# Weight scales found in groups, and low parts of weights on GpSimd, in a four-layer attention kernel

## The chip, the cores and the metric

The kernel runs on one core of one Trainium2 chip. TensorE (PE in the profile; PEld are its weight loads), VectorE (DVE), ScalarE (ACT), GpSimd (POOL) and SyncE (SP, which here only issues DMAs) each take their own queue of instructions in order. The metric is the device time of one execution, in microseconds.

## The reference, cut to what matters

```python
x = A_x                                     # (1, 2048, 512)
x = x + _A_ref(_layernorm(x), A_wqkv, A_wo) # 32 heads of 16, 8 keys at distance 0, 2, .. 14
x = x + _B_ref(_layernorm(x), B_wqkv, B_wo) # 32 heads of 16, the last 256 keys
x = x + _A_ref(_layernorm(x), A_wqkv, A_wo)
x = x + _B_ref(_layernorm(x), B_wqkv, B_wo)
return x
```

Each of the two attentions projects the normalised x with `wqkv` (512 x 1536), takes a softmax over its window and projects back with `wo` (512 x 512). All is in float32.

## The kernel before, in words

The 2048 positions are cut into eight chunks of 256. A float32 matrix product is made of three float16 ones: each factor is split into a high part and a low part (the rest), and high x high, high x low and low x high are summed. To split a weight, it is first scaled by a power of two near its largest value.

**The work is a list of tasks.** `plan.add(engine, us, function, r=, w=)` adds a task with the values that it reads and writes. Every task has a place number in the table `ORDER`, by scope and in the order in which the tasks were added; an engine takes its tasks by rising place. A negative number, -1 - place, also gives the task to its second engine (`alt=`). `plan.order()` then puts the five queues into one program and hands out buffers and PSUM banks. So `ORDER` fixes what every engine does and when. The scopes are `pA` and `pB` (the preparation of the two pairs of weights, function `prep`, line 766), `W` (110 idle tasks), and `A0`, `B0`, `A1`, ... `B15`: An and Bn are the steps of `layer_a` (line 1019) and `layer_b` (line 1184) for chunk n mod 8 of the first (n < 8) or second pair of layers.

**The idle tasks** (`idle`, line 1496) are three matmuls each on the constant `selt`, into a bank that nobody reads. `selt` is built by GpSimd at the start (lines 747 to 752), after the other constants.

**Preparation.** `prep(T)` handles four weight matrices, s = 0, 1, 2 (the three parts of `wqkv`: Q, K, V) and 3 (`wo`), each in two halves j of 128 x 1024 elements:

- `load` (line 785) brings a half to SBUF. For s < 3 it is staged in the stacks `stk[j, s]`, which B's attention uses later. For s = 3 it goes to a buffer of the pool `pp6`, which has three. A and B use the same staging, so a load for B waits until the task that last read A's half is done.
- `squares` (line 805, ScalarE or VectorE) sums the squares of each partition into one column of `am`. Its unused full output goes to the place of the low part.
- Two PE transpositions (line 818) bring the two columns of 128 sums into one row of 256 on one partition.
- `one` (lines 821 to 830), six small VectorE instructions, takes the maximum, makes a power of two of its root, and from it two factors. A PE matmul with `ones` (line 833) spreads them to 128 partitions, and `factors` (line 837) copies them into `psc`.
- For s = 1 and 3, `both_scales` (line 844) makes the product of two scales that a later step needs.
- `split` makes the high part (line 861 on ScalarE, 863 on VectorE) and then the low part (line 865, always VectorE): low = weight x factor - high, one instruction of 1024 elements (two of 512 for B's s = 0 and 1).

**Around it.** `norm` (line 876) takes statistics (L889, L892, L895), a power on GpSimd (`rstd`, L898), a shift (L901), normalises (`xnorm`, L916, into the pool `pxn` with one buffer), transposes on PE (L920) and splits (L925, L926). `proj_t` (L945 to L947) and `proj_n` (L965 to L968) are the projections; each waits for all high and low parts of its matrix. In `layer_a` the products of q and k (L1078) come in four groups of four, each summed on PE (L1086); then maximum, difference, exponential, sum, reciprocal and scaling (L1109 to L1121; in chunk 0 behind a copy, L1099, and a select, L1102), a split of the result (L1142, and the rest, `erest`, L1129), eight weighings of v (`weigh`, L1168) from PSUM banks that PE spreads, each summed over the window by `total` on VectorE (L1173) or GpSimd (L1175 to L1177), and the output projection in `finish` (L988 to L996). In `layer_b`, K and Q go through DRAM into the stacks by SyncE's DMAs (L1209, L1220); zero rows are written to the stacks once (`put`, L1487), after A's and B's staged weights have left them.

Of the kernel before, what the change touches and what calls it, by code (L numbers as in the profile page):

```python
# [10 lines left out]
BF16 = mybir.dt.bfloat16  # L11
# [4 lines left out]
ALU = mybir.AluOpType  # L16
# [24 lines left out]
    "pA": [2, -7, 1, 0, 4, 3, 7, 7, 9, 7, 13, 6, 12, 3, 2, 4, 3, 6, 8, 10, 11, 14, 22, 10, 17, 11, 18, 6, 8, 5, -9,  # L41
        15, 10, 16, 25, 20, 17, 34, 14, 27, 7, 12, 10, 15, 43, 41, 39, 59, 44, 46, 27, 53, 24, 76],
    "pB": [15, 19, 9, 18, 61, 60, 52, 72, 54, 39, 80, 29, 61, 13, 26, 14, 25, 77, 75, 60, 92, 62, 63, 35, 92, 41, 85,
        17, 23, 16, 22, 89, 69, 65, 109, 71, 43, 93, 37, 94, 18, 36, 12, 31, 102, 93, 72, 113, 74, 78, 42, 98, 40,
        84, 20, 31, 23, 3, 19, 21, 20, 22],
    "W": [12, 71, 79, 83, 101, 136, 2, 84, 100, 87, 86, 73, 137, 88, 111, 16, 0, 1, 144, 141, 90, 13, 142, 125, 105,
        124, 96, 106, 95, 104, 126, 139, 112, 98, 107, 68, 123, 91, 110, 135, 145, 14, 76, 103, 138, 119, 266, 310,
        218, 251, 239, 273, 244, 265, 260, 274, 272, 263, 275, 278, 285, 268, 269, 238, 319, 253, 256, 315, 448, 436,
        3432, 3433, 3412, 3489, 3438, 3466, 3471, 3431, 3464, 3469, 3491, 3499, 3490, 3488, 3505, 3484, 3480, 3582,
        3580, 3576, 3589, 3587, 3586, 3585, 3570, 3584, 3575, 3577, 3571, 3581, 3583, 3572, 3560, 3579, 3496, 3511,  # L50
        3512, 3502, 3588, 3578],
    "A0": [0, 0, 2, 1, 3, 4, 2, 5, 1, 5, 5, 11, 4, 9, 9, 15, 0, 1, 17, 18, 19, 20, 21, 22, 23, 24, 34, 38, 40, 42,
        46, 47, 48, 51, 13, 20, 26, 27, 28, 29, 30, 31, 32, 33, 35, 36, 37, 39, 45, 49, 50, 52, 16, 21, 54, 55, 56,
        57, 58, 63, 66, 82, 64, 65, 67, 74, 78, 80, 81, 85, 32, 33, 5, 7, 31, 30, 33, 32, 44, 38, 36, 37, 35, 53, 43,
        40, 41, 42, 62, 50, 51, 49, 48, 70, 28, 6, 55, 56, 30, 57, 58, 59, 34, -9, 94, 64, 9, 66, 10, 97, 68, 11, 67,
        -70, 108, 70, 12, 73, 14, 99, 77, 15, 75, -80, 38, 13, 114, 115, 116, 117, 118, 120, 121, 122, 81, 44, -83,
        127, 128, 129, 130, 131, 132, 133, 134, 86],
    "B0": [83, 88, 87, 89, 90, 18, 91, 46, 143, 48, 97, 45, 140, 47, 95, 147, 150, 153, 154, 155, 157, 161, 165, 151,
        156, 158, 159, 163, 164, 166, 169, 53, 103, 54, 102, 24, 25, 29, 28, 26, 27, 33, 43, 38, 40, 148, 168, 170,
        175, 180, 184, 185, 186, 149, 162, 167, 171, 174, 176, 178, 179, 56, 105, 55, 104, 30, 35, 32, 37, 34, 36,  # L60
        39, 42, 41, 44, 241, 243, 247, 249, 250, 252, 255, 258, 65, 240, 248, 257, 259, 262, 267, 270, 276, 67, 246,
        133, 226, 124, 245, 132, 222, 118, 221, 119, 237, 128, 225, 125, 242, 135, 138, -140, 140, 45, 46, 279, 68,
        288, 70, 32, 309, 280, 69, 286, 72, 33, 311, 74, 282, 152, 295, 157, 283, 149, 277, 146, 287, 154, 292, 155,
        281, 151, 284, 150, 158, 73, 160, 47, 48, 322, 82, 323, 80, 35, 397, 372, 90, 380, 91, 37, 413, 99, 318, 174,
        324, 178, 300, 161, 313, 170, 316, 172, 321, 176, 312, 171, 314, 173, 179, -181, 181, 49, 50, 411, 98, 395,
        94, 40, 458, 404, 96, 407, 97, 39, 463, 111, 299, 168, 345, 186, 379, 194, 374, 193, 353, 189, 373, 192, 344,
        185, 354, 188, 195, -197, 197, 67, 69, 432, 103, 426, 100, 41, 443, 440, 106, 439, 107, 43, 453, 109, 76, 72,
        77, 78, 258, 79, 80, 271, 270, 123, 56, 503, 504, 505, 506, 507, 508, 509, 510, 286, 83, 125, -284, 512, 515,
        516, 518, 519, 520, 521, 522, 293, 84],
    "A1": [8, 21, 24, 19, 23, 26, 4, 28, 49, 146, 50, 100, 51, 152, 52, 101, 16, 17, 160, 173, 177, 182, 187, 189,  # L70
        190, 191, 196, 197, 202, 203, 205, 207, 208, 213, 57, 60, 172, 181, 183, 188, 192, 193, 194, 195, 198, 199,
        200, 201, 204, 209, 211, 212, 58, 59, 210, 214, 216, 217, 219, 223, 228, 232, 220, 227, 229, 230, 231, 233,
        235, 236, 61, 62, 21, 23, 108, 106, 109, 107, 206, 111, 113, 110, 112, 215, 114, 115, 117, 116, 224, 122,
        120, 121, 123, 234, 126, 127, 63, 129, 130, 131, 64, 134, 254, 137, 26, 136, 25, 261, 141, 27, 142, -144,
        264, 144, 28, 145, 30, 271, 148, 31, 147, -154, 66, 29, 289, 290, 291, 293, 294, 296, 297, 298, 159, 71,
        -157, 301, 302, 303, 304, 305, 306, 307, 308, 163],
    "B1": [162, 164, 165, 166, 167, 34, 169, 75, 317, 77, 175, 76, 320, 79, 177, 328, 329, 337, 339, 341, 342, 343,
        347, 326, 327, 330, 332, 333, 334, 335, 338, 86, 187, 85, 184, 56, 55, 54, 53, 52, 51, 64, 68, 61, 71, 336,
        349, 350, 352, 356, 358, 360, 361, 340, 346, 348, 351, 355, 357, 359, 365, 87, 190, 88, 191, 57, 60, 59, 58,
        62, 63, 65, 66, 70, 73, 418, 430, 435, 438, 441, 442, 445, 446, 108, 451, 452, 455, 457, 460, 461, 462, 464,  # L80
        112, 444, 232, 233, 415, 219, 221, 416, 218, 220, 412, 212, 213, 403, 206, 207, 427, 223, 225, 433, 226, 229,
        449, 235, 237, 239, 110, 241, 74, 75, 478, 118, 476, 117, 52, 488, 470, 115, 485, 120, 53, 499, 473, 116,
        469, 114, 55, 500, 498, 124, 486, 122, 57, 525, 132, 450, 236, 240, 472, 256, 260, 459, 244, 246, 454, 242,
        247, 477, 261, 263, 467, 249, 251, 468, 252, 254, 471, 255, 259, 264, 121, 272, 81, 82, 530, 133, 524, 130,
        59, 549, 526, 131, 532, 134, 60, 550, 562, 143, 541, 137, 62, 607, 542, 139, 561, 144, 63, 608, 153, 501,
        280, 284, 523, 294, 295, 531, 296, 297, 513, 289, 291, 502, 281, 285, 487, 267, 269, 497, 275, 277, 514, 288,
        290, 298, 135, 299, 86, 87, 600, 151, 581, 148, 64, 619, 620, 158, 610, 154, 66, 636, 616, 156, 638, 162, 71,
        652, 635, 160, 627, 159, 70, 653, 169, 553, 310, 312, 554, 311, 313, 568, 315, 318, 609, 333, 335, 601, 326,
        327, 605, 328, 329, 548, 305, 308, 569, 319, 321, 336, 157, 339, 104, 105, 644, 164, 646, 165, 73, 671, 654,
        168, 657, 170, 77, 682, 658, 171, 670, 174, 78, 683, 675, 176, 669, 175, 80, 687, 179, 106, 109, 114, 115,  # L90
        387, 116, 117, -90, 403, 188, 90, 724, 725, 726, 727, 728, 729, 730, 731, 417, 120, 190, -416, 733, 734, 735,
        737, 738, 739, 742, 743, 420, 121],
    "A2": [11, 45, 47, 25, 29, 96, 19, 99, 78, 325, 83, 182, 81, 331, 84, 183, 22, 24, 362, 363, 364, 366, 367, 368,
        369, 370, 376, 385, 387, 389, 390, 392, 393, 394, 89, 93, 371, 375, 377, 378, 381, 382, 383, 384, 386, 388,
        391, 398, 399, 400, 401, 402, 92, 95, 408, 409, 410, 417, 419, 420, 424, 428, 406, 421, 422, 423, 429, 431,
        434, 437, 101, 104, 36, 42, 199, 201, 198, 200, 396, 203, 204, 202, 205, 405, 211, 209, 208, 210, 414, 215,
        216, 214, 217, 425, 222, 224, 102, 227, 228, 230, 105, 231, 447, 234, 44, 238, 45, 456, 245, 47, 243, 46,
        465, 250, 51, 248, 48, 466, 253, 50, 257, -263, 113, 49, 474, 475, 479, 480, 481, 482, 483, 484, 265, 119,
        -267, 489, 490, 491, 492, 493, 494, 495, 496, 273],
    "B2": [268, 274, 276, 278, 279, 58, 282, 126, 511, 127, 287, 128, 517, 129, 292, 527, 528, 529, 533, 534, 535,  # L100
        536, 537, 538, 539, 540, 543, 544, 545, 546, 547, 136, 300, 138, 307, 88, 89, 92, 93, 90, 91, 99, 94, 107,
        110, 552, 558, 567, 570, 571, 572, 573, 574, 551, 555, 556, 559, 560, 563, 564, 565, 147, 320, 145, 316, 95,
        101, 98, 97, 100, 96, 103, 102, 108, 111, 642, 647, 655, 659, 660, 661, 662, 665, 172, 667, 668, 672, 673,
        674, 676, 677, 679, 177, 664, 364, 366, 634, 348, 349, 639, 351, 353, 626, 344, 345, 621, 342, 343, 651, 358,
# [1433 lines left out]
```

## Time and profile before

| | us |
|---|---|
| median of the runs shown (1453.41 to 1456.76, 3 runs) | 1454.05 |
| the profiled execution's own time | 1453.95 |
| its span, from the first to the last instruction | 1451.9 |
| busy: PE / DVE / ACT / POOL | 1355.8 / 1207.2 / 735.7 / 662.3 |
| mean granted TensorE clock | 0.974 |

In rows of the timeline the first number is the start in us from the span's start and the second the busy time; `x4` is a run of four instructions; a bracket gives the idle time ahead on that engine and what ended it. In rows of groups the last parts are the busy us, the mean ns of one, and the idle time ahead. In rows of the chain that ended last, the numbers are start and length.

### The profile page before, as it was taken

The numbers are of one execution on the slowest core, as the hardware profiler recorded it, in microseconds if no ns is written. First come the engines' busy times: TensorE is split into PE (matmuls) and PEld (weight loads), VectorE is DVE, ScalarE is ACT, GpSimd is POOL, SyncE is SP. The second block draws the span as 40 slices with busy tenths as digits, with TensorE's granted clock in tenths as the row PEclk, the third lists the DMA queues.
The fourth block names the chain that finished last, engine by engine and source line by source line (L and its number), as shares of the span: only waits on it lengthen the run. The fifth ranks groups of instructions, "written<-read, shape, count | busy, mean of one in ns | idle before, by whom it ended". The sixth has DMA issues, their size and how long they took to land.

```text
span 1451.9 us, 35262 instructions
## 1 busy us (share of the span) xinstructions
PE 1355.8 (93%) x14058; PEld 792.8 (55%) x14058; DVE 1207.2 (83%) x2311; ACT 735.7 (51%) x1049; POOL 662.3 (46%) x756
## 2 busy tenths in 40 slices
PE   7798999999899998989989998999999999999998
PEld 5474645647365563746547364654647456474554
DVE  7959698797979979697887969898797988979794
ACT  6522345554554555555554444454454555545564
POOL 2505054372734618363471716356272542737333
PEclk9998999999999999999999999999999999999999
DMA  7031122212221221222122231212212132132221
GB/s 261 16 79 32 54 49 73 65 51 82 55 75 49 63 83 36 92 45 77 45 63 81 55 100 32 85 51 68 75 48 94 24 82 69 44 90 55 72 67 46
DMA packets 89221, 97.40 MB, mean 67 GB/s; under 512 B 34016, under 2 KB 60128, under 8 KB 89056
## 3 DMA queue, kind: packets, MB, share of 16 engines
q1 hardware_dynamic: 88800, 94.89, 23.5%
q8 instruction: 110, 1.80, 0.5%
q14 instruction: 55, 0.45, 0.1%
q10 hardware_dynamic: 256, 0.26, 0.1%
HBM read 50.33 MB, written 35.09 MB: 59 GB/s over the span
## 4 chain that ended last, share of the span: by engine, by line
PE 57%; DVE 24%; POOL 6%; issue 5%; ACT 3%; DMA 3%; SPq 1%; DVEq 0%; POOLq 0%; ACTq 0%
PE banks L945 10%; PE banks L947 9%; PE banks L946 9%; PE banks L1389 6%; DVE m L1281 5%; PE banks L1086 4%; DVE banks L1285 4%; DVE pw L1168 4%; PE banks L1357 3%; PE banks L967 3%; PE banks L1263 3%; PE banks L965 3%; PE banks L968 2%; PE banks L920 2%; POOL pw L1175 2%
## 5 line engine op out<-in xcount | busy, mean ns | idle before, releaser
L1363 ACT ACTIVATE p<-banks,sclB 128x768 f32<-128x768 f32 x480 | 420.6, 900 | 250.1 <-PE banks L1359 203.5
L1372 POOL TENSOR_SCALAR_AFFINE_SELECT p<-p 128x1024 f32<-128x1024 f32 x240 | 262.9, 1102 | 411.2 <-ACT p L1363 387.2
L1281 DVE TENSOR_REDUCE m<-banks 128x2 f32<-128x512 f32 x448 | 299.7, 688 | 5.2
L1285 DVE COPY_PREDICATED banks<-maskt,banks 128x256 f32<-128x256 int16 x448 | 181.4, 424 | 67.3 <-PE banks L1266 53.8
L1078 DVE TENSOR_TENSOR pr<-kv,q 128x512 f32<-128x512 f32 x232 | 164.2, 761 | 44.0 <-ACT kv L1059 16.3
L1389 PE MATMUL banks<-p,v 128*32 128x128 f32 (+1 forms) x3840 | 196.8, 331 | 3.4 <-POOL p L1372 2.5
L1357 PE MATMUL banks<-stk,stk 64*128 64x256 f16 x960 | 136.2, 281 | 27.4 <-DVE m L1281 10.3
L1389 PEld LDWEIGHTS banks<-p,v 128*32 128x32 f32 x3840 | 106.7, 109 | 98.5 <-issue 38.8
L1168 DVE TENSOR_TENSOR pw<-banks,kv 128x1024 f32<-128x1024 f32 x128 | 153.1, 1215 | 2.6 <-PE banks L1155 1.4
L1175 POOL TENSOR_TENSOR pw<-pw 128x512 f32<-128x512 f32 x101 | 129.4, 1281 | 19.8 <-DVE pw L1168 19.3
L1266 PE MATMUL banks<-stk,stk 48*128 48x128 f16 (+1 forms) x1024 | 125.6, 248 | 3.6 <-DVE m L1277 0.9
L1263 PE MATMUL banks<-stk,stk 48*128 48x128 f16 (+1 forms) x896 | 111.0, 252 | 17.4 <-DVE m L1281 7.5
L1357 PEld LDWEIGHTS <-stk 64*128 64x128 f16 x960 | 56.0, 94 | 113.6 <-issue 109.4
L1359 PE MATMUL banks<-stk,stk 64*128 64x128 f16 x960 | 108.4, 220 | 0.0
L1263 PEld LDWEIGHTS <-stk 48*128 48x128 f16 x896 | 49.7, 94 | 95.5 <-issue 91.8
L916 ACT ACTIVATE xn<-x,rs 128x512 f32<-128x512 f32 x64 | 52.1, 814 | 66.4 <-DVE rs L901 55.7
L1176 POOL TENSOR_TENSOR pw<-pw 128x256 f32<-128x256 f32 x101 | 73.9, 731 | 7.9
L1086 PE MATMUL banks<-pr,sel 128*32 128x512 f32 x512 | 70.2, 603 | 1.8 <-DVE pr L1078 1.7
L945 PE MATMUL banks<-xh,wA0h 128*128 128x256 f16 x256 | 70.3, 275 | 1.3 <-DVE xl L926 1.3
L945 PE MATMUL banks<-xh,wB1h 128*128 128x256 f16 x256 | 70.7, 276 | 0.0
L945 PE MATMUL banks<-xh,wA2h 128*128 128x256 f16 x256 | 70.5, 275 | 0.1
L947 PE MATMUL banks<-xh,wB1l 128*128 128x256 f16 x256 | 70.4, 275 | 0.0
(184 smaller groups left out, 3066.2 us busy)
## 6 DMA issues: line engine op xcount, KB each, us to landing
stk<-re SPq DMA_DIRECT2D x256, 96.0 KB
re<-eh SPq DMA_DIRECT2D x128, 128.0 KB
re<-el SPq DMA_DIRECT2D x64, 128.0 KB
oc<-os SPq DMA_DIRECT2D x120, 64.0 KB
os<-scr SPq DMA_DIRECT2D x15, 512.0 KB
x<-in_A_x_dram SPq DMA_DIRECT2D x8, 512.0 KB
xd<-x SPq DMA_DIRECT2D x16, 256.0 KB
x<-xd SPq DMA_DIRECT2D x8, 512.0 KB
```

Source lines behind the costliest of these rows:

```text
L945: nc.tensor.matmul(ps[mp].t[:, i], wh, xh, start=k == 0, stop=False)
L947: nc.tensor.matmul(ps[mp].t[:, i], wl, xh, start=False, stop=k == 3)
L1078: E.tensor_mul(pr.t, window(kv[1].t, m, 64 * tq, 64)[:, 0], qb)
L1168: nc.vector.tensor_mul(pw.t, pb.t.unsqueeze(1).broadcast_to([P, 2, W, 64]), v)
L1175: E.tensor_add(t[:, :, 0:4], t[:, :, 0:4], t[:, :, 4:8])
L1263: nc.tensor.matmul(ps.t[:, par, 0 : (2 - qb) * P], lhs, stk[hf, bef][r, col, qb * P :], start=True, stop=True)
L1281: nc.vector.tensor_reduce(out=m.t[:, :, u, qb], in_=ps.t[:, :, 0 : 2 * P], op=ALU.max, axis=AX.X)
L1285: nc.vector.copy_predicated(t[:, :, 0:P], maskt[:, 0:P].bitcast(I16).unsqueeze(1).broadcast_to([P, 2, P]), t[:, :, 2 * P : 3 * P])
L1357: nc.tensor.matmul(o[:, two], k[:, jf * P : (jf + 1) * P], q, start=True, stop=True)
L1363: nc.scalar.activation(pt.t[:, :, 2 * i : 2 * i + 2].rearrange("p s m q -> p m s q"), ps.t[:, :, : 3 * P].rearrange("p m (s q) -> p m s q" ...
L1372: nc.gpsimd.affine_select(out=v, in_=v, pattern=[[0, 8], [-1 if b == 0 else 1, P]], compare_op=ALU.is_gt if b == 0 else ALU.is_ge, fill=0. ...
L1389: nc.tensor.matmul(o, v[:, jj, 17 * h : 17 * h + 32], rhs, start=z == 0 and (b == 0 or first), stop=z == 1 and b == 1, tile_position=(0, 3 ...
```

## The change

1. **Scales in groups.** `SCALES` names the groups: for A {0}, {1} and {2, 3}, for B all four. A group of n has one `am` of 128 x n x 2. A new VectorE task `most` takes the larger of the two columns of each matrix, one transposition brings n columns to n partitions, and `one` works on n partitions at once. For n > 1 it ends with a product with the identity, which puts the n pairs of factors on a diagonal, and one matmul with n rows of ones spreads all of them. One `factors` copies them. So there are four rounds in place of eight, and no matrix of a group has its scale before all the squares of the group are there.
2. **Low parts.** The low part has GpSimd as a second engine, in two instructions: the weight is scaled in place, then the high part subtracted. `ORDER` picks it for four of the sixteen: A's s = 0, j = 1, and B's s = 2 (both halves) and s = 3, j = 1.
3. **Orders.** All tables of `ORDER` are new. Outside `pA` and `pB`, 30 tasks go from GpSimd to VectorE, 26 from VectorE to GpSimd, 12 from ScalarE to VectorE and 9 the other way. In `A0` two products and one sum go to GpSimd, and two sums and `erest` to VectorE.

```diff
 ORDER = {
-    "pA": [2, -7, 1, 0, 4, 3, 7, 7, 9, 7, 13, 6, 12, 3, 2, 4, 3, 6, 8, 10, 11, 14, 22, 10, 17, 11, 18, 6, 8, 5, -9,
-        15, 10, 16, 25, 20, 17, 34, 14, 27, 7, 12, 10, 15, 43, 41, 39, 59, 44, 46, 27, 53, 24, 76],
...
-    "W": [12, 71, 79, 83, 101, 136, 2, 84, 100, 87, 86, 73, 137, 88, 111, 16, 0, 1, 144, 141, 90, 13, 142, 125, 105,
-        124, 96, 106, 95, 104, 126, 139, 112, 98, 107, 68, 123, 91, 110, 135, 145, 14, 76, 103, 138, 119, 266, 310,
...
+    "pA": [1, 0, 2, -7, 7, 19, 8, 23, 9, 8, 16, 5, -3, 3, 2, 4, 3, 10, 27, 12, 33, 15, 19, 10, 18, 9, 17, 7, 11, 5, -12,
+        8, 12, 10, 13, 29, 58, 35, 73, 40, 25, 47, 24, 48, 41, 26, 51, 23, 46],
+    "pB": [11, 16, 13, 17, 12, 18, 14, 20, 17, 29, 18, 30, 15, 19, 16, 27, 54, 93, 59, 105, 62, 37, 74, 42, 85, 64, 40,
+        86, 36, 78, 44, -19, 38, -24, 65, 35, 87, 39, -21, 24, 29, 30, 1, 22, 20, 19, 21],
+    "W": [32, 10, 34, 24, 12, 77, 1, 82, 8, 3, 6, 13, 30, 17, 9, 35, 38, 14, 31, 129, 5, 25, 128, 75, 4, 76, 22, 28, 36,
+        21, 107, 79, 0, 26, 18, 15, 125, 2, 83, 78, 126, 37, 80, 7, 16, 11, 234, 252, 207, 258, 268, 259, 303, 240,
...
 }
+SCALES = {"A": ((0,), (1,), (2, 3)), "B": ((0, 1, 2, 3),)}
...
-    ones = cst.tile([1, P], F32, name="ones")
+    ones = cst.tile([4, P], F32, name="ones")
...
+            am = buf("psm", [P, 4, 2], F32, "am", f"am{T}{some[0]}")
...
+            def most(am=am, ax=ax, n=n):
+                nc.vector.tensor_reduce(out=ax.t[:, 0:n], in_=am.t[:, 0:n], op=ALU.max, axis=AX.X)
+
+            plan.add("DVE", 0.12, most, r=vam, w=[vax])
+            plan.add("PE", 0.3, lambda pt=pt, ax=ax, n=n: nc.tensor.transpose(pt.t[0:n, 0:P], ax.t[:, 0:n], idf), r=[vax], w=[vpt])
+
+            def one(pt=pt, a1=a1, n=n):
+
+                b = a1.t[0:n]
+                a = b[:, n]
+                nc.vector.tensor_reduce(out=a[:, 0:1], in_=pt.t[0:n, 0:P], op=ALU.max, axis=AX.X)
...
+                if n > 1:
+                    nc.vector.tensor_tensor(out=b[:, 0:n], in0=b[:, n : n + 1].broadcast_to([n, n, 2]),
+                                            in1=idf[0:n, 0:n].unsqueeze(2).broadcast_to([n, n, 2]), op=ALU.mult)
+
+            def spreads(pt=pt, a1=a1, n=n):
+                v = a1.t[0:n, 0:n] if n > 1 else a1.t[0:1, 1:2]
+                nc.tensor.matmul(pt.t[:, 2 * P : 2 * P + 2 * n], ones[0:n], v.rearrange("p a b -> p (a b)"), start=True, stop=True)
...
+                        for t, h, lo in parts:
+                            if low and which is nc.gpsimd:
+                                which.tensor_scalar(t, t, sc, None, op0=ALU.mult)
+                                which.tensor_tensor(out=lo, in0=t, in1=h, op=ALU.subtract)
+                            elif low:
+                                which.scalar_tensor_tensor(lo, t, sc, h, op0=ALU.mult, op1=ALU.subtract)
...
-                plan.add("DVE", 1.15, lambda f=split: f(None), r=[*touched[j], vsc[s], vh, vlow[j]], w=[vwt[T, s]])
+                    plan.add("DVE", 1.19, lambda E, f=split: f(E, True), r=[*touched[j], vsc, vh, vlow[j]], w=[vwt[T, s]], alt=("POOL", 3.7))
```

In the new tables pA's tasks are, in order: for each group its loads and squares, `most`, the transposition, `one`, the matmul, `factors`, and then for each matrix `both_scales` (s = 1 and 3) and the two pairs of high and low part. So the sixth number of `pA`, 19, is the place of the first transposition on TensorE, and its last, 46, that of the low part of s = 3, j = 1 on VectorE.

157 lines of the change are left out of this document (80 added, 77 removed), and 819 rows, old and new, of the table ORDER.

## The prediction

> **What bounds the kernel now.** I read the page first, then the busy times of long stretches, then the chain that ended last.
>
> ```profile
> PE 1355.8 (93%) x14058; PEld 792.8 (55%) x14058; DVE 1207.2 (83%) x2311; ACT 735.7 (51%) x1049; POOL 662.3 (46%) x756
> ...
> 0.00:90.00 90.00, 69.11 (x462) 45.28 (x463) 72.65 (x148) 48.98 (x72) 31.94 (x59) 0.94 0.38 118
> ...
> 720.00:810.00 90.00, 85.40 (x908) 49.60 (x906) 74.17 (x153) 47.87 (x68) 44.93 (x51) 0.96 0.26 69
> ```
>
> The columns of the stretches are busy us of PE, PEld, DVE, ACT, POOL, then the granted clock and the DMA share. From 90 us on TensorE is busy 85 of 90 us. Only the first 90 us, where the weights are prepared, leave it idle for 21 us. Nothing but orders changes after that, so the sum is made in those 90 us, at the marks of the chain that ended last and of the timeline:
>
> ```profile
> 52.72 1.28 POOL pw L1175
> ...
> 55.34 1.24 POOL pw L1175
> ...
> 70.18 0.80 POOL o L1177
> 71.00 0.63 ACT oh L988
> ...
> 77.37 0.71 POOL rs L898
> ...
> 84.04 0.11 PE banks L945
> ```
> ```profile
> 17.39 0.42 PE L945 MATMUL banks<-xh,wA0h 128*128 128x256 f16 x1
> ...
> 26.67 2.47 DVE L1078 TENSOR_TENSOR pr<-kv,q 128x512 f32<-128x512 f32 x4
> ...
> 34.05 2.50 DVE L1078 TENSOR_TENSOR pr<-kv,q 128x512 f32<-128x512 f32 x4 [0.23 <-PE banks L1086]
> ...
> 39.50 0.69 DVE L1078 TENSOR_TENSOR pr<-kv,q 128x512 f32<-128x512 f32 x1
> ...
> 41.36 0.58 ACT L1099 COPY e<-banks 128x512 f32<-128x512 f32 x1 [0.43 <-PE banks L1086]
> ...
> 43.02 1.08 DVE L1109 TENSOR_REDUCE mx<-e 128x64 f32<-128x512 f32 x1 [0.49 <-POOL e L1102]
> ...
> 51.43 1.21 DVE L1168 TENSOR_TENSOR pw<-banks,kv 128x1024 f32<-128x1024 f32 x1
> ```
>
> These are A0's Q projection, its first and third groups of products, its maximum, its first weighing, its sums on GpSimd (to 70.98), and B0's norm and projection. From 84 us TensorE is full, so what moves 84.04 moves the end.
>
> **What is taken away.** Durations:
>
> ```profile
> 40.10 0.40 DVE L824 TENSOR_REDUCE a1B<-banks 1x1 f32<-1x256 f32 x1
> ...
> 41.21 1.25 DVE L865 SCALAR_TENSOR_TENSOR wA3l<-stageA,pscA,wA3h 128x1024 f16<-128x1024 f32 x1
> ```
> ```profile
> L1175 POOL TENSOR_TENSOR pw<-pw 128x512 f32<-128x512 f32 x101 | 129.4, 1281 | 19.8 <-DVE pw L1168 19.3
> L1372 POOL TENSOR_SCALAR_AFFINE_SELECT p<-p 128x1024 f32<-128x1024 f32 x240 | 262.9, 1102 | 411.2 <-ACT p L1363 387.2
> ```
> ```profile
> L990 POOL TENSOR_TENSOR ol<-o,oh 128x512 f16<-128x512 f32 x1 | 1.2, 1157 | 0.0
> ```
> ```profile
> L1173 DVE TENSOR_REDUCE o<-pw 128x128 f32<-128x1024 f32 x2 | 3.8, 1918 | 0.0
> ...
> L990 DVE TENSOR_TENSOR ol<-o,oh 128x512 f16<-128x512 f32 x1 | 0.7, 693 | 0.3 <-ACT oh L988 0.3
> ...
> L837 DVE COPY pscA<-banks 128x2 f32<-128x2 f32 x4 | 0.6, 145 | 0.0
> ```
>
> One `one` holds VectorE from 40.10 to 41.21, 1.11 us. Eight become four: two of about 1.0 (half the columns) and two of about 1.15 (one product more), and four `most` of about 0.15 each are added (the copy of L837 is the nearest row): 8.9 us become 4.9. Four copies in `factors` go, 0.5. Four low parts of 1.25 go to GpSimd, 5.0. Against it, A0 takes one sum more on VectorE (1.9) and one rest (0.7) and gives two products away (1.2). VectorE so loses some 8 us of the first 90. TensorE loses twelve transpositions and four small matmuls, behind other work. On GpSimd a low part is two instructions over 1024 elements that the trace does not show. The subtraction is two of the 512-element form, 2.6 us; the scaling lies between the 1.1 of the select over 1024 elements and 2.6. So it costs 3.7 to 5.2 us, and up to 9.1 if every element goes as slowly as in the 2.27 us row below. I take 4.1, near the quiet rows.
>
> **What is moved.** The new `ORDER["W"]` holds every place from 0 to 18, and pA's first transposition has place 19: 19 idle tasks, 57 matmuls, stand ahead of it on TensorE, which takes its queue in order. Before, three tasks do.
>
> ```profile
> 7.45 2.10 PE L1498 MATMUL banks<-selt 128*128 128x256 f16 x9 [7.45 <-POOL selt L751]
> ...
> 9.35 0.89 PE L818 MATMUL banks<-idf,amA 128*1 128x128 f32 x2
> ```
> ```profile
> 57.32 1.16 PE L1498 MATMUL banks<-selt 128*128 128x256 f16 x9
> ...
> 64.23 0.61 PE L965 MATMUL banks<-wA3h,ol 128*128 128x512 f16 x1 [1.14 <-POOL ol L990]
> 64.63 0.63 PE L967 MATMUL banks<-wA3h,oh 128*128 128x512 f16 x1
> 65.06 0.63 PE L968 MATMUL banks<-wA3l,oh 128*128 128x512 f16 x1
> ...
> 69.11 1.85 PE L1498 MATMUL banks<-selt 128*128 128x256 f16 x12
> ```
>
> The idle matmuls read `selt`, which GpSimd finishes at 7.4, and nothing that the diff touches comes earlier. At half clock they start every 0.225 us (9 in 2.10, the last lasting 0.27), at full clock every 0.111. From 64.23 TensorE worked some 4.9 us before it was granted full speed. So the head of the queue is 4.9 us with 22 matmuls and 35 at 0.111, 3.9 us, and ends at 16.2; all at full clock it would end at 13.8, all at half at 20.3. The Trainium skill (TensorE: Matmul & The Clock Gate, Part 1) has the array run at half rate until about 3.4 us of sustained activity in a free-running window; by it the head would end between 15.4 and 17.1. This trace's 4.9 us agrees with the upper part.
>
> Behind the head wait the first transposition, `one` on VectorE with all that follows it there, and A0's second `xnorm` on ScalarE, since `pxn` has one buffer that the first transposes must free.
>
> **The steps,** each against its mark (ScalarE's squares, splits and copies by these rows, loads by the DMA row):
>
> ```profile
> L808 ACT ACTIVATE wA1l<-stk 128x1024 bf16<-128x1024 f32 x2 | 2.1, 1040 | 0.0
> L861 ACT ACTIVATE wA1h<-stk,pscA 128x1024 f16<-128x1024 f32 x2 | 2.2, 1140 | 0.4 <-DVE pscA L837 0.4
> L1059 ACT ACTIVATE kv<-banks 128x512 f32<-128x512 f32 x4 | 2.2, 585 | 0.0
> ```
> ```profile
> 24.00:26.00 2.00, 2.00 (x20) 1.78 (x19) 1.90 (x3) 2.00 (x4) 1.20 (x1) 1.00 1.04 310
> ```
> ```profile
> 0.81 0.46 SPq L1028 DMA_DIRECT2D x<-in_A_x_dram  x1
> ...
> 4.72 1.29 DVE L889 BATCH_NORM_STATS2 b<-x 128x6 f32<-128x512 f32 x2 [4.72 <-DMA x<-in_A_x_dram]
> ```
>
> 1. Q projection. Transposition to 16.6, `one` to 17.6, matmul behind two idle tasks and A0's transposes, factors at 18.2. ScalarE: split 18.3 to 19.5, copy, copy (second transposes done at 20.4), second split 21.1 to 22.2, VectorE's low part to 23.5. GpSimd's low part runs from 19.6 to 23.7. Start 23.8, **+6.4**.
> 2. First products. K's first half is complete after 17 tasks of three matmuls at 0.11, at 29.4, the copy at 30.0, product at 30.1; VectorE, after three low parts and four statistics, arrives there too. +3.4, so **-3.0**: two low parts and one `one` are gone, and chunk 2's x is loaded sixth, so that nothing waits for it.
> 3. Third group. ScalarE must square five halves of B's weights before it copies the second half of q and k. Their loads wait for low parts that free the staging: the first for 23.5, the next four for 25.9. At 310 GB/s a load of 512 KB takes 1.7 us; the first x, issued by 1.3, was there at 4.7, so landing adds 1.8. The fifth is there at 34.6. Two squares of 1.04 and two copies follow: 38.1, +4.0, so **+0.6**.
> 4. Maximum. Third group 2.5, three low parts 3.75 and two products 1.25 bring VectorE to 45.6; the last product to the copy of e took 1.2 us (40.2 to 41.36). But the copy stands behind B's eighth square, whose load needs the buffer that the first of these low parts frees at 41.8: there at 46.2, squared at 47.3. Copy and select to the maximum took 1.66: 49.0, +6.0, so **+2.0**.
> 5. First weighing. 8.4 us before. The 2.2 us low part and the wait behind it go; the rest on VectorE and its wait for the copy come to 1.3: 7.4 us, 56.4, so **-1.0**. B's `most` stands in this stretch ahead of the sum of e and all that follows; its last squares end near 50.2, while VectorE is still at `less` to 50.7, which hides it.
> 6. Last sum. Before 19.55 us, with six sums and one rest on GpSimd. Five sums of 2.6 and the rest, starting 1.25 after the weighing, with 0.6 for a buffer and 0.5 for contention: 16.4 us, 72.8 against 70.98, so **-3.2**.
> 7. B0's projection. The 6.4 us from 70.98 to 77.37 stay: GpSimd's low part ahead of `rstd` starts after a copy and a split (1.8 us) and ends at 5.9. Only one idle task is left between the last reduction and B0's transposes, where 34 were, so A0's first output half runs cold, 12 matmuls at 0.43 (64.63 to 65.06), 5.1 us, and pushes the second by 0.8. Low parts on both engines add 0.5 (below). **+1.3**.
>
> Sum: 6.4 - 3.0 + 0.6 + 2.0 - 1.0 - 3.2 + 1.3 = +3.1 at 84 us.
>
> ```profile
> 63.51 1.75 DVE L865 SCALAR_TENSOR_TENSOR wA3l<-stageA,pscA,wA3h 128x1024 f16<-128x1024 f32 x1
> ...
> 64.13 2.27 POOL L1175 TENSOR_TENSOR pw<-pw 128x512 f32<-128x512 f32 x1
> ...
> 92.39 2.54 SPq L1209 DMA_DIRECT2D re<-eh  x4
> ```
>
> A low part beside GpSimd work took 1.75 us for 1.25, and GpSimd 2.27 for 1.28. The Trainium skill (GPSIMD Engine Reference, 1. Specifications) says that GpSimd shares its SBUF interfaces with VectorE and contends with instructions of two SBUF inputs, which speaks against moving low parts there while others stay. These two rows agree; the contention in steps 6 and 7 is priced by them.
>
> SyncE: the zero rows of B0's stacks are queued ahead of K's writes and wait for GpSimd's last low part. `rstd` ends at 80.2; a low part of 4.1, a copy and A2's `rstd` of 0.95, and another 4.1 make 89.4, eight writes of about 0.65 follow, partly done by then, to about 93. K's writes, at 92.39 before, are ready at 95.5. Hidden by 2 us, and lost above 5.2 us for a low part.
>
> **The rest.** Outside the preparation 30 tasks go from GpSimd to VectorE and 26 back, 21 small ones move between ScalarE and VectorE, and neighbours swap places. No row prices this. Of 90 us some 5 are idle on TensorE in the steady part; a tenth of that, won or lost, in each of 15 stretches is 7 us at the most. I take 0.
>
> The profiled execution took 1453.95 us (span 1451.9 and 2.05 around it), 0.1 below the median of 1454.05. Forecast: 1453.95 + 3.1 = **1457.0**.
>
> **The rivals.**
> A. The head is shorter or hidden. For each us that the first transposition comes before 16.2 the start gains one; at 13.8 it is 1454.6, and without the loads' +0.6 and half of the +2.0 1453.0. For it: the loads, not TensorE, hold ScalarE. Against it: 7.45 is a releaser that the trace names.
> B. Faster: the new order of the later stretches wins what the start loses. TensorE's idle time is cut by 0.5 us of the 5 in each of 15 stretches, 7.5 us: 1449.5. It beats the start from 0.2 us per stretch on. Or the head costs nothing at all: the first transposition is then at 10.1, every mark 6.1 us earlier and the time 1451, 1448 if steps 3 and 4 come to nothing with it.
> C. Slower by more: the staging buffer. `pp6` has three; A's two halves of wo and B's first take them. If B's second half waits for the half whose low part comes last (after the last products, 47.1), its load lands at 51, its square ends at 52.2, and the copy of e, queued behind it on ScalarE, comes 4.9 us later: 1462. It decides only if the low part of the other half (place 46 of `pA`) does not free the buffer.
>
> **How the numbers follow.** About 0.2% (2.9 us) is what a measurement of this kernel can tell from no change. Forecast (1454.6 to 1460) 0.50, of which 0.20 lies below 1456.96; A (1451.1 to 1454.6) 0.14; B (below 1451.1) 0.19; C (above 1460) 0.17. So faster 0.19, same 0.34, slower 0.47. The range reaches to B's and C's middle and a little beyond: 1448 to 1463.
>
> **What would show it.** The head: the first transposition (L818 before) near 16, with 57 idle matmuls from 7.45, and the Q projection near 23.8; if it starts before 18, step 1 is wrong. ScalarE waiting for B's loads near 30 to 34 shows step 3. The first weighing at 56, the last sum at 73 and B0's projection at 87 show the rest. If these hold and the end does not, B is right; a copy of e near 53 shows C. A low part above 5.2 us on GpSimd, with K's writes waiting for zero rows, would make the forecast too low.

## The result, and the profile after

| | before | after |
|---|---|---|
| median (runs, range), us | 1454.63 (4, 1453.41 to 1456.76) | 1470.03 (4, 1468.98 to 1472.79) |
| profiled execution / its span, us | 1453.95 / 1451.9 | 1472.79 / 1471.1 |
| granted TensorE clock, mean of the profiled execution | 0.974 | 0.955 |

The ratio is 1.0107 (95% interval 1.0094 to 1.0120): the changed kernel is 15.6 us slower. The forecast was 1457.0, the range ended at 1463. The profiled execution of after is the slowest of its four, 18.8 us above that of before.

The same long stretches as in the prediction, in the changed kernel:

```profile
0.00:90.00 90.00, 58.75 (x382) 37.37 (x382) 67.24 (x116) 47.15 (x69) 43.93 (x61) 0.85 0.36 114
720.00:810.00 90.00, 85.37 (x918) 50.64 (x918) 75.30 (x140) 45.89 (x66) 44.16 (x50) 0.96 0.23 62
```

VectorE did get lighter in the first 90 us, by 5.4 us where some 8 were forecast (72.65 to 67.24), and GpSimd heavier (31.94 to 43.93). But TensorE did 10 us less in that time (69.11 to 58.75), and its granted clock fell from 0.94 to 0.85. The steady stretch is as full as before (85.40, 85.37).

TensorE's timeline of after. The 57 idle matmuls of the head run from 7.47; the first transposition follows at 16.38; the Q projection starts at 23.01, stops 1.13 us for GpSimd's low part and 0.47 us for one of VectorE's; B0's projection starts at 91.48, at 0.21 us per matmul, twice the 0.11 of full speed. That is what "half clock" means below:

```profile
7.47 9.07 PE L1523 MATMUL banks<-selt 128*128 128x256 f16 x57 [7.47 <-POOL selt L749]
16.38 0.27 PE L831 MATMUL banks<-idf,axA 128*1 128x128 f32 x1
...
23.01 0.27 PE L970 MATMUL banks<-xh,wA0h 128*128 128x256 f16 x1
...
25.17 0.28 PE L972 MATMUL banks<-xh,wA0l 128*128 128x256 f16 x1 [1.13 <-POOL wA0l L884]
...
27.45 0.28 PE L972 MATMUL banks<-xh,wA1l 128*128 128x256 f16 x1 [0.47 <-DVE wA1l L886]
...
91.48 0.40 PE L970 MATMUL banks<-xh,wB0h 128*128 128x256 f16 x1 [2.54 <-DVE xl L951]
...
92.24 0.42 PE L972 MATMUL banks<-xh,wB0l 128*128 128x256 f16 x1
92.45 0.42 PE L970 MATMUL banks<-xh,wB1h 128*128 128x256 f16 x1
```

VectorE's timeline, at the marks of the prediction. Low parts (L886) that take 1.27 us alone (48.60) take 2.2 on average at 23.04 and at 43.15:

```profile
23.04 4.35 DVE L886 SCALAR_TENSOR_TENSOR wA1l<-stk,pscA,wA1h 128x1024 f16<-128x1024 f32 x2
...
31.35 1.29 DVE L1103 TENSOR_TENSOR pr<-kv,q 128x512 f32<-128x512 f32 x2 [0.18 <-ACT kv L1084]
...
39.50 2.53 DVE L1103 TENSOR_TENSOR pr<-kv,q 128x512 f32<-128x512 f32 x4 [1.72 <-ACT kv L1084]
...
43.15 4.32 DVE L886 SCALAR_TENSOR_TENSOR wA2l<-stk,pscA,wA2h 128x1024 f16<-128x1024 f32 x2
...
48.60 1.27 DVE L886 SCALAR_TENSOR_TENSOR wA3l<-stageA,pscA,wA3h 128x1024 f16<-128x1024 f32 x1
...
52.07 1.04 DVE L1134 TENSOR_REDUCE mx<-e 128x64 f32<-128x512 f32 x1 [2.20 <-POOL e L1127]
...
59.51 1.23 DVE L1193 TENSOR_TENSOR pw<-banks,kv 128x1024 f32<-128x1024 f32 x1
...
79.52 1.45 DVE L886 SCALAR_TENSOR_TENSOR wB1l<-stk,pscB,wB1h 128x512 f16<-128x512 f32 x2
...
84.06 2.26 DVE L886 SCALAR_TENSOR_TENSOR wB0l<-stk,pscB,wB0h 128x512 f16<-128x512 f32 x2
86.20 3.38 DVE L886 SCALAR_TENSOR_TENSOR wB1l<-stk,pscB,wB1h 128x512 f16<-128x512 f32 x2
...
90.74 1.28 DVE L951 TENSOR_TENSOR xl<-banks,xh 128x512 f16<-128x512 f32 x2
```

GpSimd's timeline: a low part is 2.85 us of scaling (L883) and 2.12 to 2.52 of subtraction (L884), 5.0 to 5.4 together; two of A0's products (42.70) take 3.69 us together; the last sum ends at 76.26; B0's `rstd` waits behind a low part:

```profile
19.66 2.86 POOL L883 TENSOR_SCALAR stk<-stk,pscA 128x1024 f32<-128x1024 f32 x1 [10.84 <-ACT wA0h L888]
22.60 2.52 POOL L884 TENSOR_TENSOR wA0l<-stk,wA0h 128x1024 f16<-128x1024 f32 x1
...
42.70 3.69 POOL L1103 TENSOR_TENSOR pr<-kv,q 128x512 f32<-128x512 f32 x2 [2.42 <-PE banks L1111]
...
75.81 0.45 POOL L1202 TENSOR_TENSOR o<-pw 128x128 f32<-128x128 f32 x1
78.06 2.85 POOL L883 TENSOR_SCALAR stk<-stk,pscB 128x1024 f32<-128x1024 f32 x1 [1.80 <-ACT wB2h L888]
81.00 2.12 POOL L884 TENSOR_TENSOR wB2l<-stk,wB2h 128x1024 f16<-128x1024 f32 x1
83.22 0.72 POOL L923 TENSOR_TENSOR rs<-rs,mhalf 128x2 f32<-128x2 f32 x1
...
94.55 2.13 POOL L884 TENSOR_TENSOR wB2l<-stk,wB2h 128x1024 f16<-128x1024 f32 x1
```

After 92 us the distance still grows. One exponential of A (L1138 before, at 44.9 to 1311.6 us) marks each of the 16 chunks; in after the sixteen are:

```profile
L1163 ACT ACTIVATE e<-e,sclA x16: 711/722/722, 53.9 to 1324.6; 128x512 f32<-128x512 f32 x16
```

Each number is how much later the exponential of that chunk starts than before, in order: 9.0, 10.9, 12.3, 10.9, 13.2, 13.4, 13.7, 14.7, 13.1, 13.2, 12.7, 14.1, 12.5, 12.5, 11.1 and 13.0 us. The spans end 19.2 apart. So the loss of this execution comes in three parts: 9 us up to A0's maximum, 4 us from there to the steady chunks, and 6 us in the last 150 us. In that last part the closing projection waits 3.11 us for ScalarE and starts at half clock (0.43 us per matmul, then 0.21). Before, it waited 1.09 us and ran at 0.22 from its first matmul. Rows of after, and one of before:

```profile
1460.27 0.61 PE L992 MATMUL banks<-wB3h,oh 128*128 128x512 f16 x1 [3.11 <-ACT oh L1013]
...
1462.80 0.63 PE L992 MATMUL banks<-wB3h,oh 128*128 128x512 f16 x1
...
1464.09 0.38 PE L993 MATMUL banks<-wB3l,oh 128*128 128x512 f16 x1
```
```profile
1442.41 0.39 PE L967 MATMUL banks<-wB3h,oh 128*128 128x512 f16 x1 [1.09 <-ACT oh L988]
```

### The profile page after: what moved, and what is told of

The parts are those of the page before. It is cut to its first block, busy times and chain, and to the rows that moved or that the text cites. A ratio compares the mean times of both kernels' runs of the same rounds, so it can differ in the third digit from the quotient of the medians.

```text
span 1471.1 us, 35151 instructions
## 1 busy us (share of the span) xinstructions
PE 1361.9 (93%) x14038; PEld 797.9 (54%) x14038; DVE 1199.4 (82%) x2292; ACT 734.8 (50%) x1046; POOL 675.9 (46%) x758
## 4 chain that ended last, share of the span: by engine, by line
PE 31%; DVE 12%; DMA 3%; issue 3%; ACT 2%; POOL 1%; SPq 1%; ACTq 0%; POOLq 0%; DVEq 0%
PE banks L970 5%; PE banks L971 4%; PE banks L972 4%; PE banks L1414 4%; DVE m L1306 3%; PE banks L1382 2%; DVE banks L1310 2%; PE banks L992 2%; DVE pw L1193 2%; PE banks L993 2%; PE banks L1111 2%; PE banks L990 2%; PE banks L1288 2%; ACT p L1388 1%; PE banks L945 1%
## 5 line engine op out<-in xcount | busy, mean ns | idle before, releaser
L972 PE MATMUL banks<-xh,wA2l 128*128 128x256 f16 x256 | 70.5, 275 | 2.2 <-DVE wA2l L886 2.2
L970 PE MATMUL banks<-xh,wB0h 128*128 128x256 f16 x256 | 70.1, 274 | 2.5 <-DVE xl L951 2.5
L1224 DVE SCALAR_TENSOR_TENSOR el<-banks,eh 128x512 f16<-128x512 f32 x64 | 43.4, 686 | 33.9 <-ACT eh L1221 33.4
```

Source lines behind the costliest of these rows:

```text
L970: nc.tensor.matmul(ps[mp].t[:, i], wh, xh, start=k == 0, stop=False)
L972: nc.tensor.matmul(ps[mp].t[:, i], wl, xh, start=False, stop=k == 3)
```

## The experiments

All ran beside the kernel before, whose median was 1453.35 to 1455.34 on the chips used, so ratios are compared; an excess in us is the ratio's part over 1, times 1455. A bracket behind a ratio is its 95% interval; 0.001 of it is 1.5 us. Kernels named b_ start from the kernel before, best_try and the others from the changed one, except late_only (its text says how it is made). Line numbers in their rows differ by a few. Diffs of `ORDER` are given as queues.

**Where in time.** The orders are cut where both kernels have done the same 322 tasks.

```diff
 late_only:  preparation, first 322 tasks: before;  rest of ORDER:
-            before
+            after
 early_only: preparation, first 322 tasks: after;   rest of ORDER:
-            after
+            before
```

> The kernel before, with its own preparation and its own order for the first 322 tasks outside preparation (up to B0's scores, some 105 us), and the changed kernel's orders for all that follows. Theory: most of the loss is made before that point (the offset of the marks is +10.8 us at B0's exponential and +13 at the steady chunks), so the later orders alone cost 3 to 5 us: 1458 to 1460 us. Rival 1, the later orders are neutral, as predicted: 1454 to 1456. Rival 2, the later orders lose it all and a late start would have been made up: above 1464.

> The changed kernel's preparation, low parts on GpSimd and order up to the same point, then the orders of the kernel before. Theory: the start keeps its +11 us: 1464 to 1467. Rival 1 (later orders neutral): 1468 to 1471, as the changed kernel. Rival 2 (a late start is made up): 1454 to 1458.

late_only: 1459.2 us, ratio 1.0024 (1.0012 to 1.0036), +3.5 us. early_only: 1468.6, 1.0091 (1.0078 to 1.0104), +13.2. Most of the loss is made in the preparation and the orders up to the cut, as the theory had it, and it is not made up. The later orders cost the kernel before 3.5 us (1.7 to 5.2), where the prediction took 0. Taking them back from the changed kernel wins 2.4, which the intervals do not tell from nothing: early_only missed its theory (1464 to 1467) and lies in the range of the rival that calls the later orders neutral.

**The head.**

```diff
 no_head, TensorE's queue:
-idle x19, transposition of A's s = 0
+idle x3,  transposition of A's s = 0       (IDLE = 94)
 b_head:
-idle x3,  transpositions of A's s = 0
+idle x19, transpositions of A's s = 0      (IDLE = 126)
 after_selt:
     nc.gpsimd.memset(mhalf, -0.5)
+    selt = ... (its six lines, moved up from behind sel4)
```

> The changed kernel without 16 of the 19 idle tasks ahead of the first transposition (94 idle tasks in all; they compute nothing). Theory: the first transposition comes near 10 instead of 16.4, the Q projection near 17 to 18, and 4 to 6 us reach the end: 1464 to 1466. Rival, the loads of B's weights or GpSimd's low parts set the start anyway and the head was cover: under 2 us, 1468 to 1470. Rival, without those matmuls the clock drops in A0's projection and takes the gain back: Q projection at half clock, no gain at the end.

> The kernel before with 16 more idle tasks ahead of its first transpositions (126 in all) and nothing else. Theory: every mark moves by what the head is longer, 5.5 to 7 us, and nothing makes it up: 1460 to 1462. Rival, the waits for loads of B's weights in this kernel (3.85 us on ScalarE at 30) cover half of it: 1457 to 1458.

> The changed kernel, with nothing else than the constant that the idle tasks read built right behind the first three constants (ready near 4.4 us in place of 7.4). All 19 idle tasks stay at the head. Theory: the head's price is the time at which its 57 matmuls end, and they start at selt: the first transposition comes 3 us earlier, 12.5 to 13.5, and the end 2.5 to 4 us: 1466 to 1467.5. Rival, no_head's gain came from having fewer matmuls (power, clock), not from when the head ends: 1469 to 1471.

no_head: 1462.7 us, 1.0044 (1.0031 to 1.0057), so 9.2 of the 15.6 us go, more than the 4 to 6 expected. b_head: 1466.7, 1.0083 (1.0063 to 1.0103): the head alone costs the kernel before 12 us, twice what was expected. after_selt: 1466.8, 1.0075 (1.0062 to 1.0087), 4.7 us of the loss go. TensorE in after_selt:

```profile
4.56 8.80 PE L1523 MATMUL banks<-selt 128*128 128x256 f16 x57 [4.56 <-POOL selt L713]
13.20 0.27 PE L831 MATMUL banks<-idf,axA 128*1 128x128 f32 x1
```

and in no_head:

```profile
7.47 2.10 PE L1521 MATMUL banks<-selt 128*128 128x256 f16 x9 [7.47 <-POOL selt L747]
9.87 0.37 PE L829 MATMUL banks<-idf,axA 128*1 128x128 f32 x1 [0.29 <-DVE axA L826]
```

With all 57 matmuls kept and only begun 2.9 us earlier, the transposition comes 3.2 us earlier, and the loss shrinks. So the price is set by when the head ends; the rival (the number of matmuls) falls. Per us by which the first transposition moves, the end moves 1.5 us in after_selt (3.2 and 4.7) and 1.4 in no_head (6.5 and 9.2), but 1.9 in b_head (6.3 and 12.1).

**The low parts on GpSimd.**

```diff
 low_dve, GpSimd's queue:
-low parts of A (0,1), B (2,0), B (2,1), B (3,1)
 VectorE's queue:
+A (0,1) behind A (0,0); B (2,0), (2,1) behind A2's shift; B (3,1) behind A1's second rest of x
 b_low_pool: the changed kernel's two-instruction form in the kernel before;
-A (0,1), B (2,1), B (2,0), B (3,0) on VectorE
+the same on GpSimd, behind A0's rstd, A1's first copy of ha, B0's rstd, A2's rstd
```

> The changed kernel with all four low parts back on VectorE: A's behind its sibling, B's two of s = 2 behind A2's shift and that of s = 3, j = 1 behind A1's second rest of x. Theory: contention was the mis-sized term. VectorE's low parts go back to 1.25 us, the Q projection starts to flow 0.8 us earlier, B0's projection some 3.2 us earlier (88 instead of 91.5), the zero rows leave 4 us earlier: 1465 to 1467 at the end. Rival, VectorE is as full without GpSimd's help, since it has 5 us more to do: 1469 to 1471.

> The kernel before with four low parts on GpSimd and nothing else: A's s = 0, j = 1 behind A0's rstd, B's s = 2, j = 1 in the idle stretch before B0's rstd, s = 2, j = 0 behind that rstd, s = 3, j = 0 behind A2's. Theory: a low part of 5.0 us on GpSimd is ready 2 us later than VectorE's, VectorE's own low parts beside its second instruction take 2 to 3 us for 1.26, so Q and K come 1.5 to 2.5 us later and that reaches the end: 1456 to 1458. Rival, the loss seen in the changed kernel came only from where the low parts stood (ahead of B0's rstd), and VectorE's relief of 5 us wins: 1452 to 1454.

low_dve: 1465.6, 1.0070 (1.0056 to 1.0084), 5.4 us of the loss go. VectorE's low parts are back at 1.24 us, and B0's rests of x come at 84.98 in place of 90.74:

```profile
20.64 2.48 DVE L884 SCALAR_TENSOR_TENSOR wA0l<-stk,pscA,wA0h 128x1024 f16<-128x1024 f32 x2
23.04 2.48 DVE L884 SCALAR_TENSOR_TENSOR wA1l<-stk,pscA,wA1h 128x1024 f16<-128x1024 f32 x2
...
84.98 0.69 DVE L949 TENSOR_TENSOR xl<-banks,xh 128x512 f16<-128x512 f32 x1
```

b_low_pool: 1464.1, 1.0063 (1.0044 to 1.0081), +9.2 us against the 2 to 4 expected, and the rival (VectorE's relief wins) falls. VectorE's timeline there shows two losses, the first of which was not in the expectation. SyncE's loads follow, in b_low_pool and then in before:

```profile
27.93 0.69 DVE L888 BATCH_NORM_STATS2 b<-x 128x6 f32<-128x512 f32 x1 [4.92 <-DMA x<-in_A_x_dram]
...
80.97 3.31 DVE L864 SCALAR_TENSOR_TENSOR wB1l<-stk,pscB,wB1h 128x512 f16<-128x512 f32 x2
```
```profile
19.23 0.38 SPq L784 DMA_DIRECT2D stk<-in_B_wqkv_dram  x1
...
20.64 0.43 SPq L1027 DMA_DIRECT2D x<-in_A_x_dram  x1
```
```profile
15.83 0.38 SPq L788 DMA_DIRECT2D stk<-in_B_wqkv_dram  x1
...
17.24 0.43 SPq L1028 DMA_DIRECT2D x<-in_A_x_dram  x1
```

The wait for a chunk's x was 1.28 us before. That x stands on SyncE's queue behind a load into the staging that the low part on GpSimd frees, 3.4 us later than VectorE did (19.23 against 15.83): the first product comes 4.0 us late (30.67). And two halves of a low part of B take 3.31 us on VectorE beside GpSimd's subtraction, where they took 1.46 before. The distance grows at later steps (B0's projection comes 9.2 us late), so these two are not the whole.

**Both, and then the later orders.** no_head_low_dve makes both edits. no_head_low_dve_early also takes the later orders of before; best_try is the same with A's low part (0,1) left on GpSimd.

> The changed kernel with both: 16 idle tasks of the head left out, and the four low parts on VectorE. Theory: the two losses add, 7.3 and 4.4 us: 1458 to 1459, and what is left over the kernel before (3 to 4 us) is the later orders. Rival, they overlap (the head gives VectorE the time in which GpSimd is late, or the other way round): 1460 to 1462.

> The changed kernel's preparation in groups and its order up to B0's scores, without 16 idle tasks of the head and with all low parts on VectorE, and then the orders of the kernel before. Theory: head 7.3, low parts on GpSimd 4.4 and later orders 3.5 us add up to the whole loss, so nothing is left: within 1.5 us of the kernel before on the same chip. Rival 1, the groups of scales win something by themselves (VectorE's 4 us): 2 to 4 us faster than before. Rival 2, the groups and the early order lose by themselves and the sum above was chance: 3 us or more slower than before.

> As no_head_low_dve_early, but A's low part of s = 0, j = 1 stays on GpSimd (in no_head the first product came at 25.2 us, 1.5 earlier than before, with it there) and only B's three go to VectorE. Theory: the 1 to 2 us at the first product are lost again behind the four low parts of A's s = 2 and 3, so that it ends like no_head_low_dve_early. Rival, they reach the end: 1 to 3 us faster than the kernel before.

no_head_low_dve: 1456.9, 1.0020 (1.0006 to 1.0035), +2.9 us. no_head_low_dve_early: 1456.9 beside 1455.2, 1.0010 (0.9999 to 1.0021), +1.5. best_try: 1456.9 beside 1455.2, 1.0008 (0.9998 to 1.0019), +1.2. Head and low parts, 9.2 and 5.4 us one by one, take 12.7 together; the later orders are worth another 1.4. Neither the 2 us by which the sum falls short nor the 1.4 is clear of the intervals. So with the three edits taken back together the loss is gone: what the groups of scales and the early order leave cannot be told from nothing, and best_try's rival falls. In the profiled execution of no_head_low_dve_early B0's projection starts earlier than before (83.88):

```profile
81.20 0.27 PE L967 MATMUL banks<-xh,wB0h 128*128 128x256 f16 x1
```

So in that execution the groups and the early order win 2.7 us at B0, but at A's eighth chunk the exponential stands where it stood before (+0.1 us). No version that was run beats the kernel before.

**The groups alone.** b_group_b groups B's four scales in the kernel before; b_group_b2 places them better.

```diff
 SCALES (b_group_b, b_group_b2):
+{"A": ((0,), (1,), (2,), (3,)), "B": ((0, 1, 2, 3),)}
 no_head_single: no_head with
-{"A": ((0,), (1,), (2, 3)), ...
+{"A": ((0,), (1,), (2,), (3,)), ...
```

> The kernel before with B's four scales found in one group and A's one by one; each round has one transposition and one small reduction more in the place of two transpositions. B's high and low parts stand behind the group's factors; otherwise the order is that of before, with all low parts on VectorE. Theory: three rounds of 1.1 us less on VectorE, and 2.3 us of low parts leave the stretch before the first weighing, which comes 1 to 2 us earlier; all eight low parts of B then stand between 60 and 84 us, where VectorE has room beside GpSimd's sums: 1452.5 to 1454.5. Rival, the eight low parts crowd the stretch before B0's projection, as in the changed kernel: 1456 to 1459.

> As b_group_b, but placed better: the round's small instructions right behind the second weighing, only two of B's high parts ahead of the cast of the first half of the weighed sums on ScalarE (in b_group_b three, for which the cast waited 5 us), B's first low parts behind the last sum, those of V behind B0's rests of x. Theory: the loss of b_group_b (9 us) was mostly that placement: 1455 to 1458, still not faster, since eight low parts stand between the last sum and B0's projection where before had six. Rival, the rounds saved show: 1451 to 1453.

> no_head with A's s = 2 in a round of its own right behind s = 1, its high parts ahead of B's squares and its low parts behind the second group of products; s = 3 has its own round, too. Theory: the group of s = 2 and 3 put four low parts between the third group of products and the maximum (20.8 us from the first product to the maximum, against 16.4 before); with two of them gone from there the maximum comes 2 to 3 us earlier, 1460 to 1461. Rival, the same instructions are only moved and ScalarE's squares of B, now 2.3 us later, hold the maximum: 1462.5 to 1465.

b_group_b: 1464.2, 1.0063 (1.0041 to 1.0084). b_group_b2: 1463.3, 1.0050 (1.0033 to 1.0067). The first weighing did come 0.6 us earlier in b_group_b, but in both ScalarE's cast of the weighed sums stands behind B's first high parts, which wait for the group's factors. ScalarE in b_group_b2:

```profile
65.23 3.03 ACT L886 ACTIVATE wB0h<-stk,pscB 128x512 f16<-128x512 f32 x4 [11.80 <-DVE pscB L854]
68.13 0.59 ACT L1011 CAST oh<-o 128x512 f16<-128x512 f32 x1
```

The cast was at 61.24 before. In b_group_b2 the third group of products was also 4.0 us late already (38.00 against 34.05). It is my placement that costs there, so these two say nothing of the best that a group of four can do; both expectations missed. no_head_single: 1465.4, 1.0070 (1.0055 to 1.0084), 4 us worse than no_head and above the ranges of its theory and its rival. From the first product to the maximum it took 19.6 us against 20.8 in no_head and 16.4 before, a gain of 1.2 where 2 to 3 were expected, and the Q projection came 2.4 us later (the matmuls ahead of it ran at half clock longer). But after_selt and no_head_spread, which keep the group of A's s = 2 and 3, took 19.8 as well, so it is not shown that the group costs anything in that stretch.

**The clock.**

```diff
 no_head_spread: no_head, TensorE's queue:
+idle x2, x5, x4, x5 behind A0's third and fourth spread and the two halves of its output projection
 b_selt: selt moved up as in after_selt, and
-idle x3, transpositions of A's s = 0
+idle x8, transpositions of A's s = 0       (IDLE = 115)
```

> The changed kernel with the 16 idle tasks of the head moved into the stretch of A0's weighings and output projection (2, 5, 4 and 5 behind the spreads, the first and the second half of the output projection), where the kernel before has 34 and the changed one has one. Beside no_head (1462.7 us, 27 us of the first 100 at half clock) the output projection and B0's projection should run at full clock. Theory: time at half clock in the first 100 us falls to 10 to 15 us, B0's projection comes 1.5 to 3 us earlier, 1459.5 to 1461.5. Rival, sums on GpSimd and VectorE set these marks and the clock is free there: 1462 to 1463.

> The kernel before, with the constant that the idle tasks read built right behind the first three constants (ready near 4.4 instead of 7.4 us) and 8 idle tasks in place of 3 ahead of the first transposition (115 in all). Theory: the head then ends before the first sums of squares are there (9.3 us) and costs nothing, and the clock is at full speed from 8 to 10 us on in every execution: 1451 to 1454, and with less spread. Rival, the clock at the start does not matter to the end: 1453 to 1455, no difference.

no_head_spread: 1467.9, 1.0073 (1.0055 to 1.0091), not better than no_head but 4 us worse, outside theory and rival; four of its six executions are at 1467.6 to 1469.3, two at 1462.0 and 1463.2, and the profiled one, of the second kind (its marks lie within 1.2 us of no_head's up to B0), does not show why. b_selt: 1456.1, 1.0007 (0.9995 to 1.0020): no difference, its rival held. Idle matmuls placed by hand did not win time here.

## Why the prediction was wrong, step by step

| step | predicted | measured at its mark | |
|---|---|---|---|
| 1 Q projection | +6.4 | +5.6 (23.01), and 1.6 of stalls behind it | right |
| 2 first product | -3.0 | -0.9 (31.35) | low parts on GpSimd and beside it |
| 3 third group | +0.6 | +0.8 (39.50) | right, with the wait for ScalarE's copy |
| 4 maximum | +2.0 | +3.6 (52.07) | low parts beside GpSimd's products, a sum at half clock |
| 5 first weighing | -1.0 | -1.0 (59.51) | right |
| 6 last sum | -3.2 | -2.8 (76.26) | right |
| 7 B0's projection | +1.3 | +2.3 (91.48) | low parts of B, half clock |
| sum at B0 | +3.1 | +7.6 | |
| the rest | 0 | +8.0 (15.6 less 7.6) | "I take 0" |

The last of these marks is the first matmul of B0's projection, in before:

```profile
83.88 0.27 PE L945 MATMUL banks<-xh,wB1h 128*128 128x256 f16 x1
```

The direction, the head as the largest term and the place of each loss up to B0 were right. no_head and after_selt show the head. That it ended at 16.5, near the 16.2 of the forecast, is partly luck: the same 57 matmuls ended at 15.3 in low_dve. Two terms were mis-sized.

**The first is GpSimd's work in the preparation** (steps 2, 4 and 7: 4.7 us too little). Its low part was taken at 4.1 us, "near the quiet rows", and measures 5.0 to 5.4: the scaling takes 2.85 us, outside the 1.1 to 2.6 that were given for it. And contention was priced at 0.5 in step 6, 0.5 in step 7 and nothing in steps 2 and 4, while one low part of VectorE waits up to 2 us. Rows 22.60 and 23.04 show how: GpSimd's subtraction lasts from 22.60 to 25.12, and of VectorE's two low parts that begin at 23.04 the first ends at 26.2 (3.16 us), the second takes 1.27. The Trainium skill (SBUF — State Buffer, Who interferes with whom) says that a VectorE instruction with two SBUF inputs contends with a GpSimd instruction that reads SBUF, and it calls the contention an exclusive lock. For the subtraction these rows agree. Beside the one-input scaling they mostly do not: the two halves at 79.52 took 1.45 us, as they do alone (1.46 in low_dve), inside GpSimd's scaling of 78.06 to 80.91; only at 84.06 are two halves 0.8 us longer beside one. In step 4 it is two of A0's products, which the new orders put on GpSimd, that alternate with VectorE's two low parts (42.70 and 43.15). Some 0.9 us of the 4.7 is not GpSimd's: the last sum of the products took 2.53 us at half clock in after, and 1.66 in after_selt, which has the same orders:

```profile
48.13 2.53 PE L1111 MATMUL banks<-pr,sel 128*32 128x512 f32 x8 [0.21 <-DVE pr L1103]
```
```profile
44.95 1.66 PE L1111 MATMUL banks<-pr,sel 128*32 128x512 f32 x8 [0.32 <-DVE pr L1103]
```

low_dve puts the low parts' share of the end at 5.4 us; at the marks it gives back 0.7 us in step 2 and 2.7 in step 7.

**The second is "what moves 84.04 moves the end".** The end moved by twice as much. The later orders account for some 3.5 us of it (late_only): "I take 0" is the failed step, although its bound of 7 us held them. The rest, some 4.5 us, stays open. The head alone shows such a growth with the orders of before: in b_head the transposition comes 6.3 us later, A0's exponential 8.6 (53.49 against 44.91) and the end 12.1.

One candidate is the granted clock. Over 72 executions of the kernel before, the mean granted clock lies between 0.961 and 0.975 and the time between 1450.8 and 1460.2, with a correlation of -0.79 and 5.2 us per 0.01. The changed kernel's four have 0.958 on average, before's 72 have 0.970: by that slope, an estimate, 6 us, which includes the later orders' share (late_only: 0.967). But that the clock is the cause is not shown, and b_head speaks against it as the whole: its mean is 0.969 beside 0.971 for the kernel before on the same chip, 1 us by the slope, and it loses 12.1. no_head_spread, which tried to give clock back, failed.

The rivals. A (a shorter head) fell: the transposition came at 16.38. B's half on the later orders fell, late_only being slower, not faster. C's mark, the copy of e "near 53", did not come: it stood at 50.7, and ScalarE's wait for B's load hid behind a sum of products at half clock. The warning on SyncE did not come true. With the last low part ending at 96.7, the zero rows spread over 18 us and K's writes came at 101.58, 9.2 us later than before. But the zero rows ended at 99.28 and stayed hidden by 2 us, as forecast: SyncE then waited 2.2 us for ScalarE's `eh`, which comes out of the late projection. Two rows of SyncE's timeline, and its wait:

```profile
81.05 18.23 SPq L1512 DMA_DIRECT2D stk<-pad  x8
101.58 3.00 SPq L1234 DMA_DIRECT2D re<-eh  x3
```
```profile
SPq L1234 <- ACT eh L1221: 2.2, 1, 2.2
```

The prediction's range left no room for two terms missing on the same side: the GpSimd instructions had no row in the trace, and the bound of 9.1 us per low part that the text itself gave was not carried into the range.

## What to carry to other kernels

Work ahead of the first useful instruction on an in-order engine is priced by when it ends, here at 1.4 to 1.9 us of the end per us, so look at what it waits for: the idle tasks read nothing in the plan (they are added with `w=` alone), but wait for `selt` until 7.47 us on the chip. Before moving an elementwise step to GpSimd, price three things: its own instructions by a row of the same form, the two-input instructions of VectorE that will run beside it, and the DMA queues that wait for the buffer it frees; b_low_pool lost 9 us while VectorE had 5 us less to do. And check what a gain at one mark leaves at the next ones: 2.7 us won at B0 were gone by A's eighth chunk.

## What the runs showed of the hardware that was not expected

- The same 57 matmuls took 7.8 to 9.1 us in different executions (low_dve 7.84, early_only 8.32, b_head 8.37, after_selt 8.80, after 9.07). At 0.111 us each they would take 6.3 at full clock, so the array ran at half clock for 3 to 5.5 us of steady work before full speed was granted.
- The granted clock of the profile does not show this. It stands at 1.00 for the first 46 us of after, and so from 8 to 9 us, where 7 matmuls of the head run, as from 14 to 15, where 12 do. The mean clocks above do not hold the head's half clock.
- With gaps it can take longer. In the profiled no_head_low_dve the matmuls ahead of the Q projection were still at half clock at 14.90 (three in 0.85 us), 7.4 us after the first; in no_head, with the same queue on TensorE, they ran at full speed at 10.89 (six in 0.82). TensorE in no_head_low_dve:

```profile
7.45 2.10 PE L1521 MATMUL banks<-selt 128*128 128x256 f16 x9 [7.45 <-POOL selt L747]
...
12.79 2.10 PE L1521 MATMUL banks<-selt 128*128 128x256 f16 x9
...
14.90 0.85 PE L1521 MATMUL banks<-selt 128*128 128x256 f16 x3
```

  That moved its Q projection by 2.4 us (19.37 against 16.93). The Trainium skill (TensorE: Matmul & The Clock Gate, Part 1) has the clock granted by a free-running window of about 3.4 us; that the same queue is granted full speed at different times agrees with a window that does not start with the kernel.
- On GpSimd the one-input scaling of 1024 float32 elements (2.85 us) was slower than the two-input subtraction with a float16 result (2.12 us).
